# Two of fourteen output stores start among the loads instead of behind them

## The chip, the cores and the metric

The kernel runs on one core of one Trainium2 chip. The metric is device microseconds of one execution. Three runs of the kernel before gave 122.66 us in the median (122.11 to 123.96); one more execution was profiled.

## The reference

The inputs q, k and v are float32 of shape batch 8, heads 8, sequence 576, head size 64. The first stage is attention within chunks of 64 tokens:

```
q_c, k_c, v_c = q, k, v as (B, H, 9 chunks, 64, 64)
scores = q_c @ k_c^T / sqrt(64);  attn = softmax(scores)
x = (attn @ v_c), heads side by side: (B, 576, 512)
```

The second stage mixes the tokens of each batch and ends with a matrix multiplication:

```
wq = x @ w_q;  wk = x @ w_k            # 512 -> 64
W_tok = wq @ wk^T / sqrt(64)           # 576 x 576
out = relu(W_tok @ x) @ w_out          # float32 (8, 576, 512)
```

## The kernel before

**Tiling.** The eight batches go through the core one behind the other, with the stages of neighbouring batches laid into each other. For a batch, `tr` (L204) transposes q and k on VectorE (L223); `sc` multiplies them on TensorE (L237); `ex` takes the exponential on ScalarE (L252); `pv` multiplies by v (L269), which carries a column of ones for the sum; `rn` on VectorE takes the reciprocal (L281) and normalizes into `xn` (L282). Then `xt` transposes `xn` on TensorE (L293, L297), `ea` evicts it, and `pj`, `ep`, `du`, `wt`, `ew`, `gm`, `eg`, `mx` and `rl` make the token mixing and its relu. The product of W_tok with x is taken as wq times (wk^T x), so the matrix of 576 x 576 is never built. Last come `om` (L407), the multiplication by w_out for 128 output rows, and `oe` (L419), ScalarE's copy of those rows from PSUM into SBUF. There are 36 such tiles of 128 rows, nine for each pair of batches.

**Order.** Everything is written out by hand. The string ORDER lists the work of TensorE, VectorE and ScalarE in program order; each engine executes its own words in that order. TR6.0 is the first of batch 6's transposes (rows of its first two quarters), SC, EX, PV, RN, XT and so on carry batch and part in the same way, and a number behind @ is a PSUM bank. ZZ words are multiplications of zeros early in the kernel.

**Loads.** The string LOADS lists the loads in order; all are issued by POOL (GpSimd), and each word is two DMAs, one for each half of the partitions (the loop over f in `load`, L151). q and k come in parts 0-2 and 2-4 and in a tail t, which serves two batches at once; v comes in parts 0-2 and 2-4. A load reads float32 from HBM and writes float16. q and k have their own tile for each pair of batches (`qk`), v has five buffers in turn (`vt`). The bars in LOADS mark words that the program lists only after a batch's `pv` words. POOL also makes one matrix and one clear early; from 25 us on it does nothing but issue loads. `issued` holds every load's DMA in order, so `issued[-2]` is the first half of v7.2-4, the last load but one.

**Stores.** `oe` issues a store on SP's queue as soon as a group of tiles is complete: three tiles (128 partitions, 6144 B each, 768 KB) for eleven of the stores, and one tile (256 KB) for three at the end. There are fourteen. The rows to be stored lie in the memory of the `qk` tiles (`osb`, L388), pair by pair. SP executes its queue in order. The first store is remembered in `last["held"]` (L429), and at the end of the program a dependency is added to it (L468): it waits for `issued[-2]`. Since SP's queue is in order, all fourteen stores stand behind that wait. Eight small loads of w_q and w_k at the very start are SP's only other DMAs.

Of the kernel before, what the change touches and what calls it, by code (L numbers as in the profile page):

```python
# [50 lines left out]
v5.2-4 q6.0-2 k6.0-2 q6.2-4 k6.2-4 q6.t k6.t | v6.0-2 v6.2-4 q7.0-2 k7.0-2 q7.2-4 k7.2-4 | v7.0-2  # L51
v7.2-4
""".split()


@with_exitstack
def kernel(
# [55 lines left out]

    last = {}
    issued = []
    halves = [x.rearrange("b (f h) s d -> f b (h s) d", f=2) for x in (q, k, v)]

    def clear(i, eng):
        z = vt[i][:].bitcast(F32).rearrange("p g c -> p (g c)")
        e = nc.gpsimd if eng == "G" else nc.vector  # L120
        zf = zero[:].bitcast(F32)
        if eng == "A":
            nc.scalar.copy(z, zf[:, 0:1].broadcast_to([P, NG * VP // 2]))
        else:
            e.memset(z, 0.0)
        for f in range(2):
            at = f * (D + 2) + D
            rows = slice(CH * f, CH * f + CH)
            if eng == "A":
                nc.scalar.activation(vt[i][rows, :, at], zf[rows, 0:NG], AF.Exp)  # L130
            else:
                e.memset(vt[i][rows, :, at : at + 1], 1.0)

    def load(word):
        if word == "ident":
            make_identity(nc, idf[:])
            return
        if word == "clear":
            clear(NVB - 1, "G")
            return  # L140
        if word == "wout":
            for f in range(2):
                nc.gpsimd.dma_start(
                    wout[CH * f : CH * f + CH],
                    moe_w_out.rearrange("(f i p) m -> f p i m", f=2, p=CH)[f],
                )
            return
        s = "qkv".index(word[0])
        b, _, part = word[1:].partition(".")
        b = int(b)  # L150
        for f in range(2):  # L151
            rows = slice(CH * f, CH * f + CH)
            if s == 2:
                lo, hi = (int(x) for x in part.split("-"))
                d = nc.gpsimd.dma_start(  # L155
                    vt[b % NVB][rows, NCH * lo : NCH * hi, f * (D + 2) : f * (D + 2) + D],
                    halves[s][f, b].rearrange("(c p) d -> p c d", p=CH)[:, NCH * lo : NCH * hi, :],
                )
            elif part == "t":
                d = nc.gpsimd.dma_start(  # L160
                    qkt[b // 2][rows, :, s].rearrange("p b r d -> p b (r d)"),
                    halves[s][f, b : b + 2, 4 * 512 :].rearrange("b (p r) d -> p b (r d)", r=4),
                )
            else:
                lo, hi = (int(x) for x in part.split("-"))
                d = nc.gpsimd.dma_start(  # L166
                    qkm[b // 2][rows, b % 2, s, 8 * lo : 8 * hi].rearrange(
                        "p (t r) d -> p t (r d)", r=8
                    ),
                    halves[s][f, b, 0 : 4 * 512].rearrange("(t p r) d -> p t (r d)", p=CH, r=8)[  # L170
                        :, lo:hi
                    ],
                )
            issued.append(d)

    wpf = rmx[1][:].rearrange("p i n h -> p (i n h)").bitcast(F32)[:, 0 : 8 * DH].rearrange(
        "p (n c e j) -> p n c e j", n=2, c=2, e=2
# [215 lines left out]
    def place(n):  # L393
        pr, tl = divmod(n, NCH)
        at = 0
        for size in GROUPS[pr]:
            if tl < at + size:
                return pr, at, size, tl - at
            at += size
# [15 lines left out]
    def oe(n, bank, eng):  # L415
        pr, at, size, r = place(n)
        os_ = osb[pr][:, (at + r) * DM : (at + r + 1) * DM]
        if eng == "A":
            nc.scalar.copy(os_, ps[:, bank, :])  # L419
        else:  # L420
            nc.vector.tensor_copy(os_, ps[:, bank, :])
        done[pr, at] = done.get((pr, at), 0) + 1
        if done[pr, at] == size:
            row = (pr * NCH + at) * P
            d = nc.sync.dma_start(
                of[row : row + size * P].rearrange("(p r) m -> p (r m)", r=size),
                osb[pr][:, at * DM : (at + size) * DM],
            )
            if "held" not in last:  # L429
                last["held"] = d  # L430

    nc.vector.memset(zero[:].bitcast(F32), 0.0)  # L432
    for i, eng in enumerate("DDAA"):
# [3 lines left out]
    for word in LOADS[:part]:  # L437
        load(word)
# [5 lines left out]
    calls = dict(  # L444
        TR=tr, SC=sc, EX=ex, PV=pv, RN=rn, XT=xt, EA=ea, PJ=pj, EP=ep, DU=du, WT=wt, EW=ew, GM=gm,
        EG=eg, MX=mx, RL=rl, OM=om, OE=oe, WP=wp, IC=ic, ZZ=zz,
    )
    for word in ORDER:
        name, _, eng = word.partition(":")
        name, _, bank = name.partition("@")  # L450
        kind, rest = name[:2], name[2:]
        if bank:
            banks[name] = int(bank)
        args = [int(x) for x in rest.split(".")]
        if bank or kind in source:
            args.append(banks[source.get(kind, kind) + rest])
        if eng:
            args.append(eng)
        calls[kind](*args)
        if kind == "PV":  # L460
            left[args[0]] = left.get(args[0], 3) - 1
            if left[args[0]] == 0:
                while behind:
                    word = behind.pop(0)
                    if word == "|":
                        break
                    load(word)
    tc.add_manual_dep(  # L468
        last["held"].ins,
        issued[-2].ins.name,  # L470
        mybir.DependencyInfo(mybir.DependencyClass.Sync, mybir.DependencyReason.DATA),
    )


# [28 lines left out]
```

## Time and profile before

| what | value |
|---|---|
| median of three runs | 122.66 us |
| the profiled execution, its own time | 122.44 us |
| its span, first to last instruction | 120.7 us |
| TensorE busy | 103.5 us (86%) |
| VectorE busy | 73.5 us (61%) |
| ScalarE busy | 76.9 us (64%) |
| POOL busy | 78.3 us (65%) |
| moved by POOL's loads, in float16 | 14.69 MB |
| moved by SP's queue, nearly all of it stores | 9.70 MB |
| granted TensorE clock, mean | 0.975 |

The profile's page gives busy time for the whole span, then the span in 40 equal slices with the busy share of each engine in tenths, then the DMA queues, then the chain of work that ended last, then groups of instructions. A group's line gives busy time, the mean of one, and the idle time of the engine just ahead of it with what ended it. In the chain and the timelines each line begins with the start and the duration in microseconds. PE is TensorE, DVE VectorE, ACT ScalarE, POOL GpSimd; SP only issues DMAs, and "SPq" in the list of waits is its queue. The trace also gives for each DMA when it was issued and how long it took to land; landing times in the text are the sum of the two.

The loads are issued from 1.26 to 89 us and land one behind the other, the last at 94.42 us. The stores are issued from 93.40 to 116.54 us.

### The profile page before, as it was taken

What the parts mean: (1) busy time and instruction counts of PE and PEld (TensorE: products, weight loads), DVE (VectorE), ACT (ScalarE), POOL (GpSimd) and SP (SyncE); (2) the same over time, 40 slices, a digit from 0 to 9 for tenths busy, and PEclk for the clock granted to TensorE, in tenths of its full rate; (3) what the DMA queues carried; (4) which work ended last, traced back from release to release, by engine and by line L of the source; (5) the groups of instructions that cost most, each with busy time, mean ns of one, the idle gap of its engine ahead of it and who ended that gap; (6) DMA issues with size and microseconds to landing.
All of it is one profiled execution on the core that took longest, in us unless ns stands there. A gap on an engine that the chain in (4) does not pass through costs nothing.

```text
span 120.7 us, 4544 instructions
## 1 busy us (share of the span) xinstructions
PE 103.5 (86%) x1949; PEld 58.4 (48%) x1949; DVE 73.5 (61%) x128; ACT 76.9 (64%) x124; POOL 78.3 (65%) x123
## 2 busy tenths in 40 slices
PE   6909789695897897799999899999998999999940
PEld 2305265363554555455665555565555665444410
DVE  5780849954795289549955987796789286100000
ACT  7983051457375854473994896589659657868840
POOL 6998999996779889689998958889850000000000
PEclk9995999999999999999999999999999999999995
DMA  1999999999999999999999999999999899999684
GB/s 28 175 174 189 144 170 186 153 189 203 174 121 125 157 193 166 166 205 171 139 150 172 174 170 204 169 135 148 196 171 114 322 403 405 422 409 375 286 356 167
DMA packets 52115, 24.67 MB, mean 204 GB/s; under 512 B 39040, under 2 KB 50304, under 8 KB 52096
## 3 DMA queue, kind: packets, MB, share of 16 engines
q0 software_dynamic: 49440, 14.69, 117.9%
q1 hardware_dynamic: 2656, 9.70, 20.4%
q8 instruction: 15, 0.25, 0.9%
q14 instruction: 4, 0.03, 0.1%
HBM read 29.62 MB, written 9.44 MB: 324 GB/s over the span
## 4 chain that ended last, share of the span: by engine, by line
PE 43%; POOL 24%; DMA 20%; issue 4%; DVE 3%; ACT 1%; DVEq 0%; POOLq 0%
PE pb L407 21%; DMA vt<-in_v_dram 13%; POOL qk L166 11%; POOL vt L155 8%; DMA wout<-in_moe_w_out_dram 7%; POOL qk L160 5%; PE pb L237 4%; PE pb L269 4%; PE pb L316 4%; PE pb L293 3%; PE pb L369 3%; PE pb L354 2%; DVE xn L282 2%; PE pb L337 2%; DVE qkT L223 1%
## 5 line engine op out<-in xcount | busy, mean ns | idle before, releaser
L407 PE MATMUL pb<-wout,rmx 128*128 128x512 f16 x144 | 35.7, 381 | 1.7 <-DMA wout<-in_moe_w_out_dram 1.3
L223 DVE STREAM_TRANSPOSE qkT<-qk 128x512 f32<-128x512 f32 (+1 forms) x48 | 31.7, 723 | 1.8 <-DMA qk<-in_k_dram 1.6
L252 ACT ACTIVATE est<-pb 128x1024 f16<-128x1024 f32 (+1 forms) x24 | 19.1, 814 | 15.8 <-PE pb L237 15.3
L155 POOL DMA_DIRECT2D vt<-in_v_dram x32 | 27.2, 858 | 3.0 <-issue 1.9
L419 ACT COPY qk<-pb 128x512 f32<-128x512 f32 x36 | 21.2, 593 | 11.9 <-PE pb L407 11.6
L282 DVE TENSOR_TENSOR xn<-pb,rec 128x768 f16<-128x768 f32 x24 | 23.0, 957 | 0.8
L166 POOL DMA_DIRECT2D qk<-in_k_dram x32 | 19.3, 621 | 4.3 <-DMA wout<-in_moe_w_out_dram 1.7
L166 POOL DMA_DIRECT2D qk<-in_q_dram x32 | 19.3, 619 | 2.5 <-DMA vt<-in_v_dram 1.5
L383 ACT ACTIVATE rmx<-pb 128x576 f16<-128x576 f32 x32 | 19.3, 659 | 2.2 <-PE pb L369 2.1
L407 PEld LDWEIGHTS <-rmx 128*128 128x128 f16 x144 | 13.0, 104 | 14.6 <-ACT rmx L383 2.3
L237 PE MATMUL pb<-qkT 32*64 32x64 f16 x1152 | 14.1, 195 | 6.1 <-DVE qkT L223 5.2
L237 PEld LDWEIGHTS <-qkT 32*64 32x64 f16 x1152 | 11.5, 109 | 11.2 <-DVE qkT L223 8.4
L281 DVE RECIPROCAL rec<-pb 128x12 f32<-128x12 f32 x24 | 5.4, 226 | 18.0 <-PE pb L269 17.7
L269 PE MATMUL pb<-vt,est 128*64 128x130 f16 x288 | 12.4, 228 | 1.7 <-ACT rmx L383 0.8
L197 PE MATMUL pb<-zero 128*128 128x512 f16 x37 | 12.4, 467 | 1.2 <-DVE zero L432 1.2
L269 PEld LDWEIGHTS <-est 128*64 128x64 f16 x288 | 9.6, 112 | 6.6 <-issue 3.3
L293 PE MATMUL pb<-idf,xn 128*128 128x128 f32 x64 | 9.9, 281 | 0.7 <-ACT qk L419 0.3
L316 PE MATMUL pb<-xT,wpj 128*128 128x512 f16 (+1 forms) x64 | 9.6, 290 | 0.0
L293 PEld LDWEIGHTS pb<-idf,xn 128*128 128x128 f32 x64 | 7.1, 140 | 3.4 <-ACT qk L419 0.9
L354 PE MATMUL pb<-xn,wkn 128*64 128x256 f16 (+1 forms) x80 | 7.0, 281 | 0.5 <-issue 0.3
L369 PE MATMUL pb<-wqk,g 64*128 64x288 f16 x32 | 7.0, 288 | 0.1
L306 DVE COPY xT<-pb 128x640 f32<-128x640 f32 x8 | 6.5, 815 | 1.0 <-ACT xT L304 0.7
(33 smaller groups left out, 75.6 us busy)
## 6 DMA issues: line engine op xcount, KB each, us to landing
out_dram<-qk SPq DMA_DIRECT2D x11, 768.0 KB, 6.6
vt<-in_v_dram POOLq DMA_DIRECT2D x32, 144.0 KB, 5.8
qk<-in_q_dram POOLq DMA_DIRECT2D x32, 128.0 KB, 5.3
qk<-in_k_dram POOLq DMA_DIRECT2D x32, 128.0 KB, 5.3
out_dram<-qk SPq DMA_DIRECT2D x3, 256.0 KB, 2.9
qk<-in_q_dram POOLq DMA_DIRECT2D x8, 64.0 KB, 4.3
qk<-in_k_dram POOLq DMA_DIRECT2D x8, 64.0 KB, 3.7
wout<-in_moe_w_out_dram POOLq DMA_DIRECT2D x2, 256.0 KB, 7.9
```

What stands on the lines that cost most here:

```text
L155: d = nc.gpsimd.dma_start(vt[b % NVB][rows, NCH * lo : NCH * hi, f * (D + 2) : f * (D + 2) + D], halves[s][f, b].rearrange("(c p) d -> p c ...
L166: d = nc.gpsimd.dma_start(qkm[b // 2][rows, b % 2, s, 8 * lo : 8 * hi].rearrange("p (t r) d -> p t (r d)", r=8), halves[s][f, b, 0 : 4 * 5 ...
L223: nc.vector.transpose(out=to, in_=fr)
L237: nc.tensor.matmul(ps[half : half + CH, bank + i % 2, at : at + CH], lhsT=qkT[b % 2][rows, 1, tok, e], rhs=qkT[b % 2][rows, 0, tok, e], st ...
L252: nc.scalar.activation(dst, src, AF.Exp, scale=scale_attn)
L269: nc.tensor.matmul(ps[CH * o : CH * o + CH, bank + m // 3, at : at + VP].rearrange("p (f d) -> p f d", f=2)[:, :, 0 : D + 1], lhsT=est[b % ...
L282: nc.vector.tensor_tensor(out=xn[b % 2][:, 6 * u : 6 * u + 6].rearrange("p (k n) (f d) -> p k (n f) d", k=2, f=2), in0=xv[:, :, :, 0:D], i ...
L293: nc.tensor.transpose(ps[:, bank, j * P : j * P + P], src[:, at : at + P], idf[:])
L316: nc.tensor.matmul(ps[:, bank + part, 0 : at.stop - at.start], lhsT=wpj[:, c, e], rhs=xb[:, at, e], start=(c == 0 and e == 0), stop=(c == ...
L383: nc.scalar.activation(dst, src, AF.Relu, scale=scale_moe)
L407: nc.tensor.matmul(ps[:, bank, :], lhsT=c[:, r], rhs=wout[:, i, :], start=(i == 0), stop=(i == NI - 1),)
L419: nc.scalar.copy(os_, ps[:, bank, :])
```

## The change

Instead of one dependency on the first store there are three, on the first three stores. The first store waits for the second half of the load k5.2-4 (the entry in `landed` is that of the loop's last DMA), the second store for the second half of v6.0-2, and the third, with all that stand behind it in SP's queue, for `issued[-2]`, as the first one did.

```
+EARLY = ["k5.2-4", "v6.0-2"]
...
+    landed = {}
+    stores = []
...
             issued.append(d)
+            landed[word] = d
...
-            if "held" not in last:
-                last["held"] = d
+            stores.append(d)
...
-    tc.add_manual_dep(
-        last["held"].ins,
-        issued[-2].ins.name,
-        mybir.DependencyInfo(mybir.DependencyClass.Sync, mybir.DependencyReason.DATA),
-    )
+    held = [landed[word] for word in EARLY] + [issued[-2]]
+    for st, d in zip(stores, held):
+        tc.add_manual_dep(
+            st.ins,
+            d.ins.name,
+            mybir.DependencyInfo(mybir.DependencyClass.Sync, mybir.DependencyReason.DATA),
+        )
```

## The prediction

> **What bounds the kernel now.** I read the 40 slices first, for where the work changes its limit.
>
> ```profile
> PE   6909789695897897799999899999998999999940
> DMA  1999999999999999999999999999999899999684
> GB/s 28 175 174 189 144 170 186 153 189 203 174 121 125 157 193 166 166 205 171 139 150 172 174 170 204 169 135 148 196 171 114 322 403 405 422 409 375 286 356 167
> ```
>
> A slice is 3.02 us. Up to slice 30 the DMA engines carry loads alone, after it stores alone, at twice the GB/s. The page counts the bytes of the float16 side; the loads read float32, so a load's GB/s stands for twice as much traffic from HBM. The stores start so late because SP waits:
>
> ```profile
> SPq L425 <- DMA vt<-in_v_dram: 82.0, 1, 82.0
> SPq L425 <- ACT qk L419: 12.3, 8, 4.3
> ```
>
> One wait of 82.0 us, for a load of v, holds everything in SP's queue; the held load lands at 93.34 us and the first store is issued at 93.40. Then the chain that ended last, its middle and its end:
>
> ```profile
> 55.35 3.43 DMA vt<-in_v_dram
> 58.78 0.01 issue
> 58.79 1.72 DVE qkT L223 x2
> 60.50 0.04 issue
> ...
> 110.59 5.31 PE pb L407 x24
> 115.91 0.02 issue
> 115.93 0.59 ACT qk L419
> ```
>
> Up to 58.8 us the chain runs through loads and their issue on POOL. From there to 115.9 us it is TensorE almost without a hole: TensorE's idle time between 58 and 94 us, by the list of waits cut to that stretch, is 0.6 us. So in the stretch that the change touches, **TensorE sets the end**, and a load costs time exactly where it makes TensorE wait. The tail is fixed: the last eviction ends at 116.52, the last three stores are issued at 114.81, 115.68 and 116.54 and land at 118.10, 118.74 and 119.42.
>
> **What the change moves.** Two stores of 768 KB (786,432 B) each leave the burst at 93.4 us and run among the loads. Both are ready long before: ScalarE's third and sixth evictions (L419) end at 35.04 and 49.10 us. The first now goes when the second half of k5.2-4 lands (69.80), the second when that of v6.0-2 lands (82.51). Two more waits stand on SP, where a semaphore instruction takes 17 to 28 ns and nothing but stores is queued: nothing. What it costs is the DMA engines' time, and I work that out in six steps.
>
> *1. The price of a store among loads.* No row shows a store beside loads. In the burst, landings are 1.84 us apart (102.31, 104.14, 105.98, 107.80): 427 GB/s. A load of q or k is 128 KB of float16, 262,144 B of float32, and lands 0.65 us after the one ahead (q7 and k7, rows 0-2: 85.14, 85.80, 86.46, 87.10): 403 GB/s of what it reads. The two rates are so near that I take the same 16 engines to be full in both cases, and a store to push back every load behind it by its own 1.84 us. The bounds: 0 if loads leave the engines idle half the time, and 3.49 us if no load moves from a store's issue to its landing (93.40 to 96.89, the only store issued with nothing but loads ahead). I stay with 1.84, the nearest row.
>
> The Trainium skill (DMA: Bandwidth & Descriptors, section "Where 436 GB/s comes from") lets HBM bind such transfers near 358 GB/s. By that a store would cost an estimated 2.2 us, and the sum below would come out at about +2.5 us instead of +1.9. The trace speaks against it: the stores ran at 404 GB/s in the mean from 94 to 110 us.
>
> *2. The first store meets batch 6's q and k.* It is issued at 69.9 and lands near 73.4. Loads that landed from 73.2 on come 1.84 later, the second half of k6.0-2 at 77.51 instead of 75.67. VectorE's timeline shows who waits:
>
> ```profile
> 75.76 1.12 DVE L223 STREAM_TRANSPOSE qkT<-qk 128x512 f32<-128x512 f32 x1 [0.19 <-DMA qk<-in_k_dram]
> 77.34 0.23 DVE L281 RECIPROCAL rec<-pb 128x12 f32<-128x12 f32 x1 [0.46 <-PE pb L269]
> 77.61 0.96 DVE L282 TENSOR_TENSOR xn<-pb,rec 128x768 f16<-128x768 f32 x1
> 78.48 0.22 DVE L281 RECIPROCAL rec<-pb 128x12 f32<-128x12 f32 x1
> 78.74 0.96 DVE L282 TENSOR_TENSOR xn<-pb,rec 128x768 f16<-128x768 f32 x1
> ```
>
> The transpose of k for TR6.0 already waits for its load: no slack. It goes from 75.76 to 77.57 (+1.81). The 0.46 us idle behind it takes part of that, so batch 5's normalizations are 1.35 late, the last ending at 81.05 instead of 79.70. TensorE transposes their result (XT5, L293) from 80.28, so 0.58 us were to spare: TensorE is 0.77 late.
>
> *3. The lateness stays in the loads.* POOL issues a load only when the one eight places ahead has landed: q6.2-4's second half was issued at 71.85, 0.28 after v5.0-2's (71.57); k6.0-2's at 70.09, 0.29 after k5.2-4's (69.80). Its timeline shows these waits:
>
> ```profile
> 70.09 0.58 POOL L166 DMA_DIRECT2D qk<-in_k_dram  x1 [0.63 <-DMA qk<-in_k_dram]
> 71.15 1.28 POOL L166 DMA_DIRECT2D qk<-in_q_dram  x2 [0.48 <-DMA vt<-in_v_dram]
> 73.48 0.58 POOL L166 DMA_DIRECT2D qk<-in_k_dram  x1 [0.39 <-DMA vt<-in_v_dram]
> 76.87 1.69 POOL L155 DMA_DIRECT2D vt<-in_v_dram  x2 [0.34 <-issue]
> ```
>
> So loads that land 1.84 late are also replaced 1.84 late. The first issue with slack is v6.0-2 at 76.87, which the landing of q6.2-4 (76.34, plus 0.28) would have let go at 76.62: 0.25 us come back, then POOL runs back to back (7.24 us busy of 8 from 78 to 86). The loads stay 1.6 us late.
>
> *4. The second store meets batch 7's first q and k.* v6.0-2 lands at 84.1, the store goes then and is through before k7.0-2's second half, which comes 1.6 + 1.84 = 3.44 late, at 90.54 instead of 87.10. The transpose that reads it (the second of TR7.0) started at 87.85; it now starts at 90.6 (+2.75). Behind it:
>
> ```profile
> 87.00 1.71 DVE L223 STREAM_TRANSPOSE qkT<-qk 128x512 f32<-128x512 f32 x2
> 89.00 0.23 DVE L281 RECIPROCAL rec<-pb 128x12 f32<-128x12 f32 x1 [0.30 <-PE pb L269]
> 89.27 0.96 DVE L282 TENSOR_TENSOR xn<-pb,rec 128x768 f16<-128x768 f32 x1
> 90.15 0.22 DVE L281 RECIPROCAL rec<-pb 128x12 f32<-128x12 f32 x1
> 90.40 0.96 DVE L282 TENSOR_TENSOR xn<-pb,rec 128x768 f16<-128x768 f32 x1
> ```
>
> 0.30 us of idle time takes it to 2.45, so batch 6's last normalization ends at 93.81 instead of 91.36. TensorE's second part of XT6 started at 91.94, 0.58 later: **TensorE is 1.87 us late**. The 0.77 of step 2 lies inside this and isn't added: both are waits of the same TensorE for a load's clock, and the later one decides.
>
> *5. What is late next.* q7.2-4 and k7.2-4 land at 92.56 and 93.84, when VectorE, itself 2.45 late, reaches their transposes at 93.8 and 94.6. v7 lands at 96.1 (rows 0-2) and 97.9; batch 7's products (L269) then start at 97.2 and 99.6. Nothing more is added.
>
> *6. The tail.* The third store now waits until 93.34 + 3.44 = 96.8. The twelve left are 7.86 MB, 18.4 us at 427 GB/s, and behind an issue come some 1.6 us of latency (3.49 less 1.84): through by about 117, before the last one can be issued (118.4). So the burst, though it starts later, isn't the bound. Nor is anything won: the last three stores go one behind the other, and the 768 KB one among them took 3.29 us of its own. At most 0.1 us.
>
> The sum: 122.44 us, the profiled execution's own time (span 120.7, 1.7 around it), plus 1.87 is 124.3. The median of the three runs is 0.22 above that execution, so beside the median I say **124.5 us**, 1.5% slower. About 2%, 2.45 us here, is what a measurement of this kernel can tell from no change.
>
> **Rivals.** With a price D per store, steps 2 to 4 give 2D - 0.24 less the slack of 0.75, 0.30 and 0.58, that is 2D - 1.87 us, nothing below that.
> - *A store costs the loads more than its bytes.* Place: the DMA engines, at 70 to 74 and 84 to 88 us. It decides from D = 2.16, where the sum reaches 2.45. For it: eight loads of weights (32 KB each, SP's queue) run beside the first loads of q and k, and k0.0-2 lands 1.97 us behind its predecessor instead of 0.65, 1.3 us for at most 0.2 MB, far more than their bytes. Against: those come in pieces of 512 B, a store's are 6144 B. Taking D halfway to 3.49, 2.67 us, it is +3.5: 126.1. Where the forecast fails I think it fails here: slower by over 2%. The Trainium skill's figure of step 1 would belong to this case too.
> - *The loads leave room and the stores fit in.* For it: from 78 to 94 us loads land at 148 and 147 GB/s, against 191 from 71 to 78, so there are holes; the step from k6.t to v6.0-2 is 2.0 us (79.68 to 81.68). Against: the loads that matter (k6.0-2, q7, k7.0-2) come in runs with 0.65 us between them. One store absorbed of two gives nothing to +0.2; both, with 0.1 won in the tail, 122.5. I say 122.5 to 123.6.
> - *Faster by over 2%.* It would need 2.45 us out of the 2.9 between the last issue and the last landing, of which a 256 KB store took 2.06 by itself (113.95 to 116.01). No row offers that. Nor do I see the change failing to act: both stores are ready, and SP holds nothing ahead of them.
>
> **Chances and range.** The forecast, D from 1.7 to 2.15 (124.2 to 125.1): 0.43. More than its bytes: 0.36. Stores absorbed: 0.18. Faster by over 2%: 0.03. So faster 0.03, same 0.61, slower 0.36. The range goes from 122.4 to 126.2, D from nothing to 2.67; it leaves out the dearest part of the second case and the last.
>
> **What would show it.** Right: SP issues at about 69.9 and 84.1 and then from 96.8; the wait of TR6.0 for k grows from 0.2 to some 2 us; TR7.0 waits some 2 us for k where it waited for nothing; TensorE shows new idle time ahead of XT5 and XT6, 1.9 us together, and ends near 117.8; the last v lands near 97.9. Wrong: landings around 72 and 86 us that keep 0.65 us apart with a store in flight (step 1), loads that catch up by v6 (step 3), or a last store that lands less than 2.7 us behind its issue (step 6).

## The result and the profile after

The changed kernel is slower. Six runs gave 127.84 us in the median (125.06 to 129.99) against 122.5 for the kernel before (six runs, 122.11 to 123.96). The ratio is 1.029 with an interval of 1.022 to 1.037. A second set of six runs gave 128.05 (126.71 to 130.40) against 122.5 (19 runs), ratio 1.037 (1.027 to 1.047). A ratio in this text leaves out the runs that lie more than 1.5% above the fastest of their kernel, and the medians do not; the changed kernel scatters more than the one before (1.029 rests on its runs of 125.06 and 125.76 us, and the profiled one is not among them), so both numbers are given.

The profiled execution of the changed kernel took 127.21 us, with a span of 125.2 against 120.7. Its page, in the same 40 slices (of 3.13 us now):

```profile
PE   6929997888987897999998998899649999999940
PEclk9996799999999999999999999999975699999996
DMA  2999999999999999999999999999999999147684
GB/s 30 178 174 191 156 183 181 157 198 200 168 123 156 189 173 166 205 172 141 161 186 156 225 291 191 119 141 250 240 169 86 377 406 412 72 188 317 251 335 168
```

Two things are new. The GB/s rise to 291 and 250 in the two places where a store now runs among the loads. And TensorE has a hole in slices 29 and 30, where before it had 9s, with a granted clock (PEclk) of 0.7, 0.5 and 0.6 at its end and behind it (slices 30 to 32). SP's waits, who waited for whom (total, times, longest):

```profile
SPq L431 <- DMA qk<-in_k_dram: 61.0, 2, 57.4
SPq L431 <- DMA vt<-in_v_dram: 27.3, 2, 14.1
SPq L431 <- ACT qk L425: 17.6, 8, 9.4
```

The one wait of 82.0 us has become three: the stores are issued at 68.13, 82.80 and then from 96.51 us, as the change says. Who pays is seen on VectorE. Its timeline at batch 6's first transposes and at batch 7's:

```profile
73.44 0.71 DVE L229 STREAM_TRANSPOSE qkT<-qk 128x512 f32<-128x512 f32 x1 [0.33 <-DMA qk<-in_q_dram]
76.44 1.11 DVE L229 STREAM_TRANSPOSE qkT<-qk 128x512 f32<-128x512 f32 x1 [2.28 <-DMA qk<-in_k_dram]
...
87.13 0.71 DVE L229 STREAM_TRANSPOSE qkT<-qk 128x512 f32<-128x512 f32 x1 [0.92 <-DMA qk<-in_q_dram]
90.34 1.10 DVE L229 STREAM_TRANSPOSE qkT<-qk 128x512 f32<-128x512 f32 x1 [2.50 <-DMA qk<-in_k_dram]
91.29 0.17 DVE L287 RECIPROCAL rec<-pb 128x12 f32<-128x12 f32 x1
91.50 0.96 DVE L288 TENSOR_TENSOR xn<-pb,rec 128x768 f16<-128x768 f32 x1
```

In brackets stands the idle time ahead of an instruction and what ended it. TR6.0 waited 0.19 us for k before and 2.28 now; TR7.0 waited for nothing and now 0.92 for q and 2.50 for k. What that does to TensorE, by its timeline:

```profile
78.62 0.70 PE L243 MATMUL pb<-qkT 32*64 32x64 f16 x63 [0.70 <-DVE xn L288]
...
89.52 0.29 PE L375 MATMUL pb<-wq,g 64*128 64x288 f16 x1
92.51 0.39 PE L375 MATMUL pb<-wqk,g 64*128 64x288 f16 x1 [2.69 <-DVE xn L288]
92.51 0.42 PE L375 MATMUL pb<-wq,g 64*128 64x288 f16 x1
92.86 1.11 PE L299 MATMUL pb<-idf,xn 128*128 128x128 f32 x4
...
96.52 1.89 PE L413 MATMUL pb<-wout,rmx 128*128 128x512 f16 x4
```

The same place in the kernel before, from MX5.3 on:

```profile
90.52 0.28 PE L369 MATMUL pb<-wqk,g 64*128 64x288 f16 x1
90.52 0.28 PE L369 MATMUL pb<-wq,g 64*128 64x288 f16 x1
91.13 0.66 PE L293 MATMUL pb<-idf,xn 128*128 128x128 f32 x4 [0.33 <-ACT qk L419]
...
93.28 1.04 PE L407 MATMUL pb<-wout,rmx 128*128 128x512 f16 x4
...
95.28 0.54 PE L269 MATMUL pb<-vt,est 128*64 128x130 f16 x12
```

In the changed kernel TensorE stands still for 0.70 us and for 2.69 us. Behind the second wait everything is slow: four transposes take 1.11 us (0.66 before), four multiplications by w_out 1.89 us (1.04 before). The busy times of the engines, three stretches of the changed kernel and then one of the kernel before, give the granted clock in the last column but two:

```profile
86.00:92.30 6.30, 3.81 (x46) 1.91 (x45) 2.85 (x5) 3.28 (x6) 3.66 (x5) 1.00 1.26 258
92.30:99.30 7.00, 6.79 (x84) 3.81 (x84) 3.70 (x6) 3.40 (x5) 0.00 (x0) 0.51 1.45 192
99.30:110.00 10.70, 10.70 (x171) 6.31 (x170) 5.37 (x11) 7.05 (x13) 0.00 (x0) 1.00 0.73 293
```

```profile
92.30:99.30 7.00, 7.00 (x201) 4.57 (x200) 4.11 (x8) 4.54 (x7) 0.00 (x0) 1.00 0.90 304
```

From 92.3 to 99.3 us the clock is 0.51. (The counts, 84 matmuls against 201, don't compare: the same stretch of time holds other work in the two kernels.) **The 4.5 us of span** can be laid out between fixed points of TensorE's work. MX5.3, the matmul pair behind the wait, starts at 92.51 instead of 90.52: 1.99 us. From there to PV7.0 it takes 7.27 us (to 99.78) instead of 4.76 (90.52 to 95.28): 2.51 us, the low clock. From PV7.0 to the last matmul it is 20.64 and 20.63: nothing. The 1.99 us would be larger from an equal start: this execution came to TR4.0 at 54.66, 1.83 us ahead of the one before, long before the first early store. So the waits cost some 3.8 us here and the low clock 2.5, and the early start hides 1.8 of the two together. This is the account of one execution, with a mean clock of 0.951; the runs at 125.06 and 125.76 us had 0.968 and 0.970 and left no trace.

### The profile page after: what moved, and what is told of

It is laid out like the page before. It is cut to its first block, busy times and chain, and to the rows that moved or that the text cites. A ratio compares the mean times of both kernels' runs of the same rounds, so it can differ in the third digit from the quotient of the medians.

```text
span 125.2 us, 4540 instructions
## 1 busy us (share of the span) xinstructions
PE 107.7 (86%) x1949; PEld 59.9 (48%) x1949; DVE 73.6 (59%) x128; ACT 77.3 (62%) x124; POOL 78.2 (62%) x123
## 4 chain that ended last, share of the span: by engine, by line
POOL 33%; DMA 32%; PE 23%; issue 5%; DVE 3%; ACT 0%; DVEq 0%; POOLq 0%
DMA qk<-in_k_dram 17%; POOL vt L160 14%; POOL qk L171 13%; PE pb L413 12%; DMA wout<-in_moe_w_out_dram 6%; POOL qk L165 5%; DMA vt<-in_v_dram 5%; DMA qk<-in_q_dram 4%; PE pb L299 2%; PE pb L322 2%; PE pb L243 2%; PE pb L375 2%; DVE xn L288 2%; PE pb L360 1%; PE pb L275 1%
## 5 line engine op out<-in xcount | busy, mean ns | idle before, releaser
L413 PE MATMUL pb<-wout,rmx 128*128 128x512 f16 x144 | 36.5, 388 | 0.9 <-ACT rmx L389 0.5
L203 PE MATMUL pb<-zero 128*128 128x512 f16 x37 | 13.5, 504 | 1.2 <-DVE zero L437 1.2
L275 PE MATMUL pb<-vt,est 128*64 128x130 f16 x288 | 12.5, 229 | 1.9 <-ACT rmx L389 0.8
L275 PEld LDWEIGHTS <-est 128*64 128x64 f16 x288 | 9.6, 112 | 6.5 <-issue 3.1
L299 PE MATMUL pb<-idf,xn 128*128 128x128 f32 x64 | 11.0, 300 | 0.3 <-DVE xn L288 0.3
L299 PEld LDWEIGHTS pb<-idf,xn 128*128 128x128 f32 x64 | 7.6, 150 | 3.3 <-DVE xn L288 1.0
L322 PEld LDWEIGHTS <-wpj 128*128 128x128 f16 x64 | 4.8, 99 | 5.5 <-issue 1.1
L375 PE MATMUL pb<-wq,g 64*128 64x288 f16 x32 | 7.4, 296 | 0.0
```

Source lines behind the costliest of these rows:

```text
L275: nc.tensor.matmul(ps[CH * o : CH * o + CH, bank + m // 3, at : at + VP].rearrange("p (f d) -> p f d", f=2)[:, :, 0 : D + 1], lhsT=est[b % ...
L299: nc.tensor.transpose(ps[:, bank, j * P : j * P + P], src[:, at : at + P], idf[:])
L375: nc.tensor.matmul(ps[:, bank + h, 0:HS], lhsT=g16[b % 2][CH * h : CH * h + CH, i * P : i * P + P], rhs=src[CH * h : CH * h + CH, half * H ...
L413: nc.tensor.matmul(ps[:, bank, :], lhsT=c[:, r], rhs=wout[:, i, :], start=(i == 0), stop=(i == NI - 1),)
```

## The experiments

For the price of a transfer among loads I use two stretches between landings in the profiled execution of each run. Stretch A goes from the first half of v5.0-2 to the second half of k6.2-4 and contains the first early store; B goes from the second half of v6.0-2 to the second half of k7.2-4 and contains the second. Without a transfer in it, A was 7.4 to 8.5 us in six executions (mean 7.86) and B 7.3 to 8.9 (mean 8.03).

| in the stretch | A, us | B, us |
|---|---|---|
| one store of 768 KB, five executions each | 9.30 to 10.45, mean 9.89 | 10.30 to 11.13, mean 10.68 |
| longer than without | 2.03 | 2.65 |
| one store of 256 KB (e5_small) | 8.12 | 9.34 |
| two stores of 768 KB (e6_four) | 12.90 | 12.68 |
| a read of 768 KB (e7_read) | 10.63 | 12.32 |

**One store at a time.** Theory: an early store pushes back the loads behind it, and TensorE waits for them. The rival was its size; a second question was whether the losses add.

```
-EARLY = ["k5.2-4", "v6.0-2"]
+EARLY = ["k5.2-4"]          # e1_first
+EARLY = ["v6.0-2"]          # e2_second
+EARLY = ["k7.2-4"]          # e3_late
```

> Only the first store is early (behind k5.2-4); the second waits with the rest. In the profile of the changed kernel the loads around a store came about 2.6 us later, not 1.84. Theory 'dear': a store costs the loads 2.6 us. Then TR6.0's k is 2.6 late, TensorE loses 2.6 - 1.07 = 1.5 us ahead of XT5, batch 7 asks for less (2.6 - 1.87 = 0.7), and the kernel takes about +1.5 us. Theory 'own bytes': 1.84 us, TensorE loses 0.8, +0.8 us. If the loss of the change were TensorE's clock alone, it would depend on whether the wait of TensorE is long enough to lower the granted clock: with 0.8 to 1.5 us of waiting I expect no lower clock, so about 0.97 as before.

> Only one store is early, behind v6.0-2. Batch 6 is as before; batch 7's first q and k come later by the price. 'Dear' (2.6 us): TensorE loses 2.6 - 1.63 = 1.0 us ahead of XT6, +1.0 us. 'Own bytes' (1.84): +0.2 us. With e1 this also tells whether the two losses add (e1 plus e2 equal to the whole) or whether the lateness adds and the slack is paid once (whole larger than the sum: 3.3 against 2.5 with 'dear').

> One store is early, behind k7.2-4, where only the loads of v7 follow; these have 2.6 and 3.3 us to spare before TensorE's products with v. All theories in which an early store costs time through loads that TensorE waits for: no loss, between -0.2 and +0.2 us, with v7's last load 1.8 to 2.6 us later. If an early store costs by itself (through SP's queue or memory traffic at large): about half of the change's loss, +1.5 us.

Measured: e1_first 124.32 us in the median of four runs (123.62 to 126.02), ratio 1.013 (1.004 to 1.022). e2_second 124.28 in the median of ten (122.39 to 126.68), ratio 1.007 (1.001 to 1.013, from four of the ten). e3_late 122.92 in the median of ten (120.94 to 123.95), ratio 0.998 (0.991 to 1.005, from four of the ten). The kernel before had 122.40 in the same set. In their traces, TR6.0 waits in e1_first (1.29 us for q, 1.48 for k) and not in e2_second. TR7.0 waits in both: 1.95 us for k in e2_second, and 1.06 and 0.35 in e1_first, whose only early store had landed 10 us before. In e3_late the list of TensorE's waits shows nothing above 0.4 us. So no price of an early store by itself is seen. It costs where the loads behind it are waited for. The whole (3.6 to 4.5 us by the ratios) is more than e1_first and e2_second together (1.6 and 0.9), but the intervals are too wide for that alone, and part of the whole is the low clock, which neither of the two traces has behind its waits. The waits themselves say it: TensorE waits 3.39 us for late normalizations at SC6.0 and MX5.3 in the whole (0.70 and 2.69), 0.88 in e1_first (0.17 and 0.71) and 0.27 in e2_second. The lateness of the loads adds, and the slack is there only once.

**Bytes, size and direction.** First a third of the bytes per early store, then twice as many stores, then reads of the same size in place of the stores.

```
-GROUPS = [[3, 3, 3], ...
+GROUPS = [[1, 1, 1, 3, 3], ...                                   # e5_small
...
+EARLY = ["k5.2-4", "k5.2-4", "v6.0-2", "v6.0-2"]                 # e6_four
...
+    spare = [sb.tile([P, 3 * DM], F32, ...) for i in range(2)]   # e7_read
...
+                    nc.sync.dma_start(spare[len(reads)][:], src.rearrange("(p m) -> p m", p=P))
...
-    for st, d in zip(stores, held):
+    for st, d in zip(reads + stores, held):
```

> The first pair's stores are cut as 1, 1, 1, 3, 3 tiles instead of 3, 3, 3, so the two early stores are 256 KB each, a third of the bytes (sixteen stores in all). If a store's price goes by its bytes (2.2 to 2.6 us for 768 KB, so 0.75 to 0.85), batch 6 has 1.07 us of slack for it and loses nothing, batch 7 is 1.4 late with 1.3 us of slack: 0 to +0.3 us against before, no half clock. If an early store has a price of its own whatever its size, the loss stays near the change's, +3 us.

> Two stores at each of the two places instead of one. If the price goes by bytes, the two stretches lengthen by 4.2 and 5.4 us and the loads' lateness of 9.6 us, less some 1.6 us of slack paid once, is TensorE's loss: +8 us, with half clock behind the waits about 2 us more. If an early store has a fixed price per place (switching between queues), nothing changes against the change: +3.5 to 5.5 us. If the loads have room that one store uses up, the second costs more than the first.

> All stores wait for the last load but one, as before; in place of the two early stores SP issues, behind the same two loads, two reads of the same size and shape (128 partitions, 6144 B each, from q in HBM into a spare tile that nothing uses; 1.5 MB more traffic in all). In the runs so far a store lengthened the stretch from v5.0-2 to k6.2-4 by 2.1 us and the one from v6.0-2 to k7.2-4 by 2.7 us, more than its 1.84 us. Theory 'direction': writing to HBM among reads costs extra; a read costs its bytes at the loads' 403 GB/s, 1.95 us, in both stretches, and the kernel loses about 1 us less than the change, +2 us. Theory 'any transfer': reads lengthen the stretches by the same 2.1 and 2.7 us and the kernel is as slow as with the change, +3.5 us or more.

Measured: e5_small has the ratio 0.999 (0.993 to 1.006), but that rests on three of ten runs; the median is 124.7 (122.38 to 125.61), and seven runs lie at 124.2 to 125.6. Its profiled execution, one of the three, still shows the wait on TensorE:

```profile
DVE qkT L229 <- DMA qk<-in_k_dram: 3.4, 2, 2.2
PE pb L375 <- DVE xn L288: 1.4, 1, 1.4
```

So "no loss" isn't shown for e5_small; it loses less than the change. e6_four: 133.19 us (131.48 to 133.57, four runs), ratio 1.086 (1.080 to 1.093), 10.5 us: what the theory of bytes expected with the low clock added. Two stores lengthen A by 5.0 and B by 4.7 us, some 2.4 us each, so neither a fixed price per place nor room that one store uses up fits. e7_read: 128.48 us (127.79 to 130.85, four runs), ratio 1.050 (1.046 to 1.055). In its one trace the reads are dearer than the stores, 2.8 us in A (little above the dearest store's 2.6) and 4.3 in B. "Direction", in which a store costs extra because it writes to HBM, falls with that: a read was not cheaper. Why a store among loads costs 2.0 to 2.7 us when it takes 1.84 in the burst stays open; the executions scatter so much that A alone doesn't tell 2.03 from 1.84, while B's 2.65 is clear of it.

The Trainium skill (DMA: Bandwidth & Descriptors, section "Issuing engines are not separate DMA queues") says that all DMAs run on the same 16 engines and interleave, whichever engine started them; stretches A and B, 2.03 and 2.65 us longer, agree. The 358 GB/s that the Trainium skill gives on the same page, in the section "Where 436 GB/s comes from", would make a store's price an estimated 2.2 us. That lies inside what was measured here, but it has no answer to the 4.3 us of the read in B.

**A place with room?** The second rival of the prediction pointed to the 2 us ahead of v6.0-2's landing.

```
-EARLY = ["k5.2-4", "v6.0-2"]
+EARLY = ["k6.2-4"]
```

> One early store, behind k6.2-4, so that it runs while the four small tails land and in the 2 us hole ahead of v6.0-2's landing (1.2 us more than a load of v needs). Theory 'room where POOL is the limit': the hole takes up about 1.2 us of the store, the loads of batch 7 are 1.0 to 1.4 us late, within 1.3 us of slack: 0 to +0.3 us, less than e2_second's loss. Rival 'no room anywhere': loads 2.4 us late, +1 us as in e2_second.

Measured: 124.34 us (123.97 to 125.53, four runs), ratio 1.021 (1.016 to 1.027). From k6.2-4 to the second half of v6.2-4 the loads took 8.66 us, against 5.8 to 7.0 without a store there (five executions, mean 6.3): 2.3 us late, the full price. In this execution the hole takes up nothing, and v6 itself comes late for TensorE (PV6.0 waited 1.1 us). The rival falls. A likely reason, not tested: POOL issues only when an earlier load has landed, so a hole in the landings isn't room.

**The clock.** Theory: the 2.7 us wait itself lowers TensorE's clock. I filled it with multiplications of zeros.

```
-MX5.2@5 OM19@0 ... MX5.3@3 XT6.0@0
+MX5.2@5 OM19@0 ... MX5.3@3 ZZ12@7 XT6.0@0        # e4_fill
+MX5.2@5 OM19@0 ... ZZ10@7 MX5.3@3 XT6.0@0        # e4b_fill
```

> The changed kernel with twelve multiplications of zeros (512 columns, some 0.21 us each) on a free PSUM bank ahead of XT6.0, where TensorE waited 2.7 us. In the changed kernel's profile the granted clock fell to half for 6.8 us just behind that wait. Theory 'clock': the waiting itself lowers the clock; with the filler it stays at full speed there, no run is much above the others, and the time is that of the waits alone, about +3.3 us. Rival: the clock falls by chance and has nothing to do with the wait; then some runs stay 2 to 4 us above the others, and the filler adds up to 0.5 us where the wait is shorter than the filler.

> The changed kernel itself once more, for its spread and a second trace. Waits of TensorE: about 0.7 us ahead of SC6.0 and 2.5 to 2.7 us ahead of MX5.3 (its PSUM bank is read by RN6.1, which stands behind the late TR7.0). Theory 'clock': in every run that has a wait above some 2.5 us there, the granted clock is at half behind it for a multiple of 3.4 us, and the runs lie at 125 to 130 us by how long that lasts. Rival 'chance': the lower clock is missing in this trace although the wait is there.

> The changed kernel with ten multiplications of zeros (512 columns, a free PSUM bank), this time ahead of MX5.3, where TensorE really waits: in e4_fill the 3.0 us wait stood ahead of the filler, which then ran at half clock in 4.05 us, so that run only added work. Ten take some 2.1 us at full clock and lie inside the wait. Theory 'clock': no half clock between 80 and 110 us, no run above 126.5, about 125 to 126 (the waits alone, +3 us). Rival 'chance': as many runs at 127 to 130 as without the filler.

e4_fill was misplaced by one instruction: 130.92 us (130.47 to 131.40, four runs), ratio 1.070 (1.063 to 1.078). Its timeline of TensorE:

```profile
94.71 0.40 PE L375 MATMUL pb<-wqk,g 64*128 64x288 f16 x1 [3.04 <-DVE xn L288]
94.72 0.42 PE L375 MATMUL pb<-wq,g 64*128 64x288 f16 x1
95.07 4.05 PE L203 MATMUL pb<-zero 128*128 128x512 f16 x12
98.96 0.60 PE L299 MATMUL pb<-idf,xn 128*128 128x128 f32 x4
```

The wait stands ahead of MX5.3, not of XT6.0, and the filler comes behind it at the low clock, 338 ns each. With the filler ahead of MX5.3, e4b_fill's timeline and its clock in 40 slices are:

```profile
93.73 2.33 PE L203 MATMUL pb<-zero 128*128 128x512 f16 x10
96.00 0.29 PE L375 MATMUL pb<-wqk,g 64*128 64x288 f16 x1
96.00 0.29 PE L375 MATMUL pb<-wq,g 64*128 64x288 f16 x1
96.22 0.66 PE L299 MATMUL pb<-idf,xn 128*128 128x128 f32 x4
```

```profile
PEclk9995899998699999999999999999999999999999
```

The filler takes 233 ns each, and the four transposes behind it 0.66 us as before the change, in place of 1.11. There is no low clock from slice 12 on. e4b_fill ran in 125.97 us (124.87 to 127.81, four runs), ratio 1.022 (1.011 to 1.033), beside 128.05 and 1.037 (1.027 to 1.047) for the changed kernel in the same set. The traces show the mechanism; the size of the gain is not shown, since the intervals overlap, and two of the four runs lie above the 126.5 us that was expected as their limit. The profiled one (127.81) has no low clock there but stops of TensorE for "issue" (0.58 and 1.54 us), of which the last section tells. after_again's profiled execution has a wait of 3.15 us at the same place and half clock for 6.8 us behind it. e6_four's has 3.9 us and the same. Waits of 0.7, 1.1 and 1.4 us ahead of MX5.3 (e1_first, e10_hole, e5_small) have none. In e7_read shorter stops than 2.69 us were enough:

```profile
80.06 0.21 PE L245 MATMUL pb<-qkT 32*64 32x64 f16 x1 [1.57 <-DVE rec L289]
81.08 0.79 PE L245 MATMUL pb<-qkT 32*64 32x64 f16 x63 [0.80 <-DVE xn L290]
...
93.97 0.36 PE L277 MATMUL pb<-vt,est 128*64 128x130 f16 x5 [1.92 <-issue]
```

```profile
PEclk9995999999999999999999999679975699999999
```

The clock is at half for 3.4 us from 81.5 us on, where 1.57 and 0.80 us of standing still lie together, and for 6.8 us from 95.2 on, behind the 1.92 us. So e7_read's time holds more of the low clock than the changed kernel's, and the price of a read goes by the stretches A and B alone. But the low clock is not all of the scatter: two runs of after_again with a mean clock of 0.973, about that of the kernel before, took 127.51 and 128.59 us.

**The tail.** Two variants of the last stores, the one with e3_late's early store, the other on the kernel before.

```
-OM33@1 OE32:A OM30@0 OE33:A OM35@1 OE30:A OM34@0 OE35:A OE34:A
+OM30@1 OE32:A OM33@0 OE30:A OM35@1 OE33:A OM34@0 OE35:A OE34:A   # e9_both
...
-[3, 3, 1, 1, 1]]
+[3, 1, 1, 1, 1, 1, 1]]                                           # e8_fine
```

> One early store behind k7.2-4 (no loss in e3_late), and the last three tiles' order changed: tile 30, which completes the last 768 KB store, ahead of tile 33, so that this store goes one tile earlier and only 256 KB stores follow. Before, the last three stores landed one behind the other, 118.10, 118.74, 119.42, behind that 768 KB store, issued at 114.81; at 113.95 it would land at 117.2 and the last 256 KB store, issued at 116.54, at 118.6 to 118.9 (it needs 2.06 alone). Theory 'tail is a queue of stores': -0.5 to -0.8 us against before. Rival 'tail is fixed by the last eviction and a store's latency of 2.9 us': no difference.

> The kernel before, with the last pair's stores cut as 3 and six single tiles instead of 3, 3, 1, 1, 1. Before, the last three stores landed behind a 768 KB store issued at 114.81, the last one 2.88 us behind its issue; single tiles are evicted 0.86 us apart and need 0.61 us of the DMA engines each, so the last one should land some 2.1 to 2.3 us behind its issue: -0.6 us. Rival 'latency': as in e9_both, where the last one still took 2.69 us, no difference that can be measured.

e9_both: 122.2 us (121.27 to 122.91, ten runs), ratio 1.001 (0.996 to 1.005). e8_fine: 122.15 us (120.58 to 123.29, twelve runs), ratio 0.997 (0.993 to 1.001). Neither is shown to beat the kernel before. In e8_fine the last seven stores land at 114.88, 115.51, 116.14, 116.78, 117.40, 118.05 and 118.70: 0.62 to 0.65 us apart, the time of 256 KB in the burst. By these landings the DMA engines work without a gap up to the end, so the last store waits in a queue that the whole burst filled. Both variants together, an early store behind k7.2-4 and single tiles at the end, were not tried.

## Why the prediction was right, and where it fell short

The sign, the place and the way were right: the time came out above the median of before and at the upper end of the range (1.029 times 122.66 us is 126.2). The size was not. 1.87 us were forecast, and by the ratios it is 3.6 to 4.5, beyond the case that got the greatest chance (0.43 for 124.2 to 125.1). The medians (127.84 and 128.05 us) and the second set's ratio (1.037 gives 127.2) lie above the range. That the first set's ratio ends just at its upper end is in part luck: that end was made from a dear store alone, without the low clock that is part of the loss.

- *Step 1, the price of a store, is the term that was mis-sized.* 1.84 us were taken; 2.03 and 2.65 were measured. With these, steps 2 to 4 give 4.68 - 0.24 - 1.63 = 2.8 us. This is the first rival, for which 0.36 was given: it decides from 2.16 us per store, and the mean is 2.34. What I gave for it, the weights beside the first loads, pointed the right way. Nor did a store pass in some 3.5 us (69.9 to 73.4), as step 2 has it: the two took 7.66 and 7.12 us from issue to landing, with loads landing in between.
- *Step 2*: right that TR6.0 waits (2.28 us by the trace), wrong in who waits behind. Not XT5 waited but SC6.0, 0.70 us: it writes a PSUM bank that RN5.2 reads.
- *Step 3, that lateness stays*, held. From v5.0-2 to the last load it was 23.6 us before; 28.0 and 28.7 in the two traces of the changed kernel.
- *Step 4* named XT6 with 0.58 us to spare. MX5.3 comes earlier: it writes banks 3 and 4, where PV6.1's result waits for RN6.1. Before, RN6.1 ended at 90.23 and MX5.3 began at 90.52, so there were 0.29 us. With that the sum of the waits is 3.1 us.
- *A term was missing*: no step asked what TensorE does behind a wait. In the profiled execution the low clock cost 2.51 us. The waits alone, from an equal start, cost 3.8 us beside the sum's 3.1.
- *Steps 5 and 6* held for the change: the last load of v landed at 96.94 without TensorE waiting for it, and the last store landed 2.88 us behind its issue in both kernels. That "the burst isn't the bound" was too strong; e8_fine shows the queue reaching the end.
- *The other rivals*: room for the stores falls with e10_hole and the two stretches. Nothing pointed to faster.

## What to carry to other kernels

A store that is ready early isn't free to go early: among loads that follow each other without room, it delayed all behind it here by 2.0 to 2.7 us, where its own time in a burst was 1.84, and each of two such delays was carried on to the end of the loads. Look for the first load behind it that an engine waits for, and for slack count PSUM banks too: the next matmul that writes a bank may wait for a late reader before any data is missing. If the wait falls on a busy TensorE, add what the lower clock behind it costs (2.51 us in the profiled execution here).

## What the runs showed of the hardware

- At or behind waits of 2.69, 3.04, 3.15 and 3.9 us TensorE ran at half its clock for 3.4 us (once) or 6.8 us (three times); in e7_read 1.92 us were enough, and 1.57 and 0.80 us close together. No limit for a single wait follows: in e10_hole the half clock came at 27.04 us, behind stops of 0.62, 0.41 and 0.74 us only, and waits of 1.1 and 1.4 us elsewhere had none behind them. The Trainium skill (TensorE: Matmul & The Clock Gate, section "HAM oscillation — how this bites in real kernels") gives as an abstract rule that idle gaps of TensorE should not exceed some 3.4 us; here shorter ones were enough.
- A read of 768 KB by SP among the loads lengthened them by 2.8 and 4.3 us, a store of the same bytes by 2.0 and 2.7.
- In nine of the fourteen traces TensorE stops for "issue" inside the products with v (L275; L277 in e7_read, L269 in e8_fine), always ahead of the same few matmuls: in batch 5's before the last 4, in batch 6's before the last 5. The stops are 0.64 us in e1_first and e2_second, 1.54 in e4b_fill and 1.92 in e7_read; in the kernel before the same place has 0.06 us. The line of e2_second, in which the early store had landed at 88.47:

```profile
88.86 0.36 PE L275 MATMUL pb<-vt,est 128*64 128x130 f16 x5 [0.64 <-issue]
```

The page counts 15 packets of instructions among the DMAs, and one (16 KB) starts at 86.52 us in that trace. In every such stop the matmuls go on 2.25 to 2.54 us behind the start of such a packet (2.34 here, and 2.28 in the kernel before), so TensorE seems to wait for instructions. An early store isn't needed for it: e3_late stops for 0.42 us at 77 us, 14 us ahead of its early store, and e8_fine, without one, for 0.34. Whether transfers among the loads make the stops longer was not tested.
